# A first stage folded twice: sixteen small tiles in one round, with mirrored rows

## The chip, the core and the metric

The kernel runs on one core of a Trainium2 chip (trn2). The metric is the device time of one execution in microseconds (us); less is better. A core has TensorE (PE in the profile, with its weight loads as PEld), VectorE (DVE), ScalarE (ACT), GpSimd (POOL) and SyncE (SP). Each engine works off its own instructions in the order in which the program gives them, and semaphores make one wait for another. POOL and SP also issue DMA transfers.

## The reference

```python
# x: (8, 3008, 256), filt_r and filt_i: (1505, 256)
X = np.fft.rfft(x, axis=1)
Y = X * (filt_r + 1j * filt_i)[None]
y = np.fft.irfft(Y, n=3008, axis=1)          # per batch and channel
h = y.reshape(24064, 256) @ w_in             # w_in: (256, 2048)
g = 0.5 * h * (1.0 + erf(h / sqrt(2)))
out = g @ w_out                              # w_out: (2048, 256), out: (24064, 256)
```

So each of the 8 batches goes through a Fourier transform along its 3008 rows, a product with a filter, and the transform back; then all 24064 rows (tokens) go through two dense layers with a GELU between them.

## The kernel before

**The transform.** 3008 is 47 x 64. Row number 64 n + w of a batch is row n (0 to 46) at column w (0 to 63). The first stage (`s1`) transforms over n for every w, the second (`s2`) over w with the twiddle factors in its tables; the product with the filter (`s2_out`, `s2_sum`, VectorE) comes next, and `s3` and `s4` transform back. Between stages the data change their layout through DRAM: `s1` writes R1, `r1` loads b_sb from it; `s3_out` writes R2, `r2` loads d_sb from it, and `s4` writes y into a ring that holds two batches.

**The first stage before.** `load_x_pairs` brings w and w + 32 of a batch into x_sb, in two partition groups of 47 rows (from partitions 0 and 64), with the rows of the second half turned by 23. `fold` (lines 109 and 110) adds and subtracts the two halves, 1024 elements per partition and operation, so that even and odd outputs need one real table each, T1s. `s1` runs four times a batch (c = 0 to 3), each time as eight matmuls with 47 rows, 64 columns of weights and 512 columns of data, into four PSUM banks: one of the tag h, three of the tag f. Two of the banks are copied out by VectorE (line 327), two by ScalarE (line 325).

**The dense layers.** Tokens go in 47 blocks of 512 (`NT`). For block t, `mm1` makes 16 products of 128 hidden columns x 512 tokens (line 640, two matmuls each), in a ring of three PSUM banks of tag h, and ScalarE applies the GELU (line 643). The second layer of the block before, `mm2_seven`, uses Strassen's seven products in place of eight: 112 matmuls of 128 columns (line 714), seven per slot. VectorE forms the sums that it needs: `sums_1` (line 685, four a block), `sums_2` (line 691, two) and `sums_3` (line 696, two), and adds its results out of two PSUM banks of tag o (lines 729 to 743); POOL sends them to the output (line 761).

**The order.** The program is written out by hand in slots, 16 to a block; a slot is one `mm1` (two matmuls) and seven matmuls of `mm2_seven`. `put(slot, f, ...)` places the steps of the next batch's transform between them; a step is issued ahead of its slot's matmuls. Batch b's tokens start in block b * 3008 // 512, and `hi = first(b)` is that block's first slot. For batches 3 to 6 the four groups of `s1` stand at `hi - 94 + (0, 3, 7, 11)`, for batch 7 four slots earlier; the folds stood 20, 13, 8 and 6 slots ahead of `hi - 94`. The loads of batch b + 1 are placed in the second stage of batch b (`load_next`): a small copy on POOL (`gate`) waits until VectorE has made a certain product, and the loads stand behind it in POOL's queue. `busy` and `crowd` keep `s4` off the slots of other stages.

Of the kernel before, what the change touches and what calls it, by code (L numbers as in the profile page):

```python
# [10 lines left out]
ALU = mybir.AluOpType  # L11
FP32 = mybir.dt.float32
BF16 = mybir.dt.bfloat16
# [5 lines left out]
NA, NB = 47, 64  # L19
K1 = 24  # L20
HB = 32
# [6 lines left out]
def _dram(src, off, dims):  # L28
    return dataclasses.replace(src, offset=src.offset + off, ap=[list(d) for d in dims])


class _Mix:
    def __init__(self, ctx, tc, x, filt_r, filt_i, w_in, w_out, out):
        self.tc, self.nc = tc, tc.nc
        self.x, self.filt_r, self.filt_i = x, filt_r, filt_i
        self.w_in, self.w_out, self.out = w_in, w_out, out
        self.B, self.S, self.D = x.shape
        self.DFF = w_in.shape[1]
        assert self.S == NA * NB and self.D == 256 and self.DFF == 2048
        pool = lambda name, bufs, **kw: ctx.enter_context(tc.tile_pool(name=name, bufs=bufs, **kw))  # L40
        P = bass.MemoryType.PSUM
        self.const = pool("const", 1)
        self.px = pool("px", 1)
        self.pa = pool("pa", 3)
        self.pb = pool("pb", 2)
        self.pp = pool("pp", 3)
        self.pd = pool("pd", 3)
        self.pool = pool
        self.po = pool("po", 4)
        self.py = pool("py", 1)  # L50
        self.pg = pool("pg", 2)
        self.pq = pool("pq", 1)
        self.small = pool("small", 1)
        self.dram = pool("dram", 2, space=bass.MemoryType.DRAM)
        c = self.const
        self.T1 = c.tile([2 * NA, 96], BF16, name="T1")
        self.T2p = c.tile([128, K1, 2, 2, 16], BF16, name="T2p")
        self.xs = c.tile([128, 4, 256], BF16, name="xs")
        self.U = c.tile([128, 2, 2 * HB], BF16, name="U")
        self.T4c = c.tile([96, NA, 2], BF16, name="T4c")  # L60
        self.F = c.tile([128, 2, K1, 256], BF16, name="F")
        self.Fu = c.tile([128, 2, 2, 6, 256], BF16, name="Fu")
        f = self.F.rearrange("p t k c -> p (t k c)")
        self.s4_sb = f[:, 0:2048].bitcast(FP16).rearrange("p (i n) -> p i n", i=8)
        self.v_sb = [f[:, o:o + 1024].rearrange("p (c d) -> p c d", c=2) for o in (2048, 3072)]
        self.T4a = f[0:96, 4096:7168].rearrange("p (w m) -> p w m", w=HB)
        self.w_in_sb = c.tile([128, 2, self.DFF], BF16, name="w_in_sb")
        self.w_out_sb = c.tile([128, 16, self.D], FP16, name="w_out_sb")
        self.w_sums = c.tile([128, 4, 8, 128], FP16, name="w_sums")
        self.ps, self.st = {}, {}  # L70
        self.flip = 0
# [11 lines left out]
    def load_x(self, lo=0, n=32, hs=(0, 1)):  # L83
        nc = self.nc
        if lo == 0 and 0 in hs:
            xt = self.px.tile([128, HB, 256], BF16, tag="x", name="x_sb")
            self.st[0, "x"], self.st["x1"] = xt[0:2 * NA], xt.rearrange("p (h w) c -> p h w c", h=2)
        xt, o = self.st[0, "x"], NA
        xv = self.x[0].rearrange("(n1 h w) d -> h n1 w d", h=2, w=HB)
        for w in range(lo, lo + n, 8):  # L90
            for h in hs:
                nc.gpsimd.dma_start(out=xt[h * o:h * o + NA, w:w + 8, :], in_=xv[h][:, w:w + 8, :])  # L92

    def load_x_pairs(self, b, c, h, n=1):

        xt = self.st["x1"]
        xv = self.x[b].rearrange("(n1 h w) d -> h n1 w d", h=2, w=HB)
        for v in range(2):
            for to, at, m in ((0, 23, 24), (24, 0, 23)) if h else ((0, 0, NA),):
                w = 16 * v + 4 * c  # L100
                self.nc.gpsimd.dma_start(out=xt[64 * v + to:64 * v + to + m, h, 4 * c:4 * c + 4 * n, :],  # L101
                                         in_=xv[h][at:at + m, w:w + 4 * n, :])

    def fold(self, b, c):

        x, tt = self.st["x1"], self.nc.vector.tensor_tensor
        k, n = slice(4 * c, 4 * c + 4), 64 + NA
        s = self.st[b, "s", c] = x[:, 0, 4 * c - 4:4 * c] if c else self.xs
        tt(out=s[0:n], in0=x[0:n, 0, k], in1=x[0:n, 1, k], op=ALU.add)
        tt(out=x[0:n, 1, k], in0=x[0:n, 0, k], in1=x[0:n, 1, k], op=ALU.subtract)  # L110
# [33 lines left out]
    def load_next(self, b, p, c, h):  # L144

        if b == 1 and c > 1:
            self.gate(self.st[b, "d", 0][0:1, 0, 0:1])
        else:
            self.gate(self.st[b, "p", p][0:1, p % 2, 1, 0, 0:1])
        self.load_x_pairs(b + 1, c, h)  # L150

    def load_w_in(self):
        wi = self.w_in.rearrange("(dc p) j -> p dc j", p=128)
# [178 lines left out]
    def table_1_tiles(self, g):  # L332
# [4 lines left out]
        for p in (0, 64):  # L337
            for r in (0, K1):
                v.tensor_copy(out=self.T1s[p:p + NA, r:r + K1].rearrange("p (u c m) -> p u c m", c=4, m=2),
                              in_=self.T1[0:NA, r:r + K1].rearrange("p (c u m) -> p u c m", u=3, m=2))  # L340

    def table_2_parities(self):

        t = self.T2.rearrange("p k r (s j e) -> p k r s j e", s=2, e=2)
        for odd in range(2):
            for d in range(2):
                for q in range(2):
                    self.nc.gpsimd.tensor_copy(out=self.T2p[64 * d:64 * d + 64, odd::2, :, q, :],
                                               in_=t[0:64, odd::2, :, q, :, odd ^ d ^ q])
# [150 lines left out]
    def r2(self, b, c):  # L500
        d = self.pd.tile([96, 8, 256], BF16, tag="d", name="d_sb")
        self.st[b, "d", c] = d
        R2 = self.st[b, "R2"].rearrange("(r w) u a k m c -> r (u a k m) w c", r=2)
        for r in range(2):
            self.nc.sync.dma_start(out=d[r * 48:r * 48 + 48, :, :], in_=R2[r][:, 8 * c:8 * c + 8, :])


    def s4(self, b, grp, half, eng):
# [274 lines left out]
def kernel(  # L783
# [9 lines left out]
    m = _Mix(ctx, tc, x, filt_r, filt_i, moe_w_in, moe_w_out, out)  # L793
    nc, B, S = tc.nc, m.B, m.S
# [3 lines left out]
    g = m.small  # L798
    wide = ctx.enter_context(ExitStack())
    m.psum(wide, w=(2, 1), m=(1, 1), n=(5, 1))  # L800
    act = "act"
# [108 lines left out]
    at = {}  # L910

    def put(slot, f, *a):
        at.setdefault(slot, []).append((f, a))

    def first(b):
        return (b * S // TCH) * 16

    busy, crowd, after = set(), set(), {}
    for b in range(1, B):
        hi = first(b)  # L920
        e = 4 * (b == B - 1)
        s1, n1, r1 = (4, 3.3, 17) if b == 1 else (hi - 87, 3.7, hi - 73) if b == 2 else (hi - 94 - e, 3.7, hi - 80 - e)
        s2 = (27, 41, 54) if b == 1 else (hi - 74, hi - 59, hi - 44) if e else (hi - 64 + (b == 2), hi - 48, hi - 32)
        busy.update(range(s1 - 1, s1 + int(3 * n1) + 2))
        for c in range(4):
            slot = (4, 8, 11, 13)[c] if b == 1 else s1 + int(c * n1)
            put((0, 1, 5, 8)[c] if b == 1 else (70, 74, 86, 94)[c] if b == 2 else hi - 94 - (20, 13, 8, 6)[c], m.fold, b, c)
            put(slot, m.s1, b, c)
        for u in range(3):
            put(r1 if u < 2 else s2[0] + 1, m.r1, b, u)  # L930
            put(s2[u], m.s2, b, u)
            for i in range(4):
                put(s2[u] + 2 * i + (b == 2 and u == 0), m.s2_out, b, u, i // 2, i % 2)
            for i in range(2):
                put(s2[u] + (9 + i if 1 < b < B - 1 else 7 + 2 * i), m.s2_sum, b, 2 * u + i)
            s3 = s2[u] + ((11, 11, 12)[u] if b == 1 else 12 if e or (b, u) in ((2, 0), (B - 2, 2)) else 13)
            put(s3, m.s3, b, u)
            put(s3 + 1, m.s3_out, b, u, 1)
            busy.update(range(s2[u] - 1, s2[u] + 5), range(s3 - 1, s3 + 2))
        after[b] = s3 + 4  # L940
        crowd.update(range(s2[0], after[b]), range(s1 + 66, s1 + 94))
        if b + 1 < B:
            for i, (u, o, p) in enumerate(((0, 5, 1), (0, 7, 1), (1, 1, 2), (1, 5, 3), (1, 7, 3), (2, 1, 4), (2, 5, 5), (2, 7, 5))):
                put((76, 77, 80, 81)[i - 4] if b == 1 and i > 3 else s2[u] + o, m.load_next, b, p, i // 2, i % 2)
# [27 lines left out]
    put(9, m.table_u_pick, g)  # L972
    put(9, m.table_4_rows, g)
    put(9, m.weights_4, g)
    put(23, m.table_u)
    put(49, m.table_4_factors, g)
    for t, slot in ((3, 67), (5, 98)):
# [17 lines left out]
    for s in range((NT + 1) * 16):  # L995
        t, jc = s // 16, s % 16
# [3 lines left out]
        if t - 1 in seven:  # L1000
            n = lambda i: (14 * i if i < 3 else 42 + 70 * (i - 3) // 13) if t == late else 7 * i
            m.mm2_seven(t - 1, n(jc), n(jc + 1))
        elif t < 2:
            n = lambda i: max(4 * i - 40, 0) if i < 16 else min(24 + 8 * (i - 16) // 3, 64)
# [36 lines left out]
```

## Time and profile before

| | us |
|---|---|
| timed runs, median of 3 | 733.9 (733.84 to 733.96) |
| profiled execution, span of its instructions (the page gives no whole time for it) | 732.0 |
| PE busy | 713.6 |
| DVE busy | 597.0 |
| ACT busy | 576.5 |
| POOL busy | 286.2 |

The span runs from the first to the last instruction of one profiled execution. Rows of the profile name a line of the kernel, the engine, the operation, the tile written and the tiles read. "busy" is the time in which at least one instruction of the engine was being executed; a time in square brackets is idle time just before an instruction, with what ended it. Instructions overlap, so that the time from one start to the next can be shorter than an instruction's own duration: the first is what it takes of its engine's queue.

The first stage's matmuls (line 429) are 224, for seven batches (batch 0 goes another way), with a median of 376 ns each; they start between 39.2 and 562.0 us. The first stages of batches 3 to 7 begin at 199.5, 288.2, 377.1, 465.7 and 550.6 us.

### The profile page before, as it was taken

The numbers are of one execution on the slowest core, as the hardware profiler recorded it, in microseconds if no ns is written. First come the engines' busy times: TensorE is split into PE (matmuls) and PEld (weight loads), VectorE is DVE, ScalarE is ACT, GpSimd is POOL, SyncE is SP. The second block draws the span as 40 slices with busy tenths as digits, with TensorE's granted clock in tenths as the row PEclk, the third lists the DMA queues.
The fourth block names the chain that finished last, engine by engine and source line by source line (L and its number), as shares of the span: only waits on it lengthen the run. The fifth ranks groups of instructions, "written<-read, shape, count | busy, mean of one in ns | idle before, by whom it ended". The sixth has DMA issues, their size and how long they took to land.

```text
span 732.0 us, 22073 instructions
## 1 busy us (share of the span) xinstructions
PE 713.6 (97%) x9016; PEld 505.9 (69%) x9165; DVE 597.0 (82%) x1091; ACT 576.5 (79%) x1050; POOL 286.2 (39%) x546
## 2 busy tenths in 40 slices
PE   7999999999999999999999999999999999999997
PEld 4846675676777666666677667666677767777776
DVE  8975698899878998798976999779988897775666
ACT  7997778688877888778887788877888788877773
POOL 7853377864223452135511364115531121121121
PEclk9999999999999999999999999999999999999999
DMA  9886544765355553646535455355545442411011
GB/s 158 160 173 161 155 89 123 201 124 100 88 169 143 120 112 107 178 99 134 128 107 162 114 132 119 97 149 151 110 102 135 141 117 84 114 47 42 30 59 59
DMA packets 81254, 87.72 MB, mean 120 GB/s; under 512 B 13393, under 2 KB 61137, under 8 KB 81153
## 3 DMA queue, kind: packets, MB, share of 16 engines
q0 software_dynamic: 22288, 39.50, 24.3%
q1 hardware_dynamic: 58449, 46.62, 23.8%
q8 instruction: 71, 1.16, 0.7%
q14 instruction: 30, 0.25, 0.1%
q10 hardware_dynamic: 416, 0.20, 0.1%
HBM read 54.00 MB, written 46.66 MB: 138 GB/s over the span
## 4 chain that ended last, share of the span: by engine, by line
PE 86%; DVE 4%; DMA 4%; issue 2%; POOL 2%; ACT 1%; DVEq 0%; POOLq 0%; ACTq 0%
PE ps_o L714 38%; PE ps_h L640 38%; PE ps_s L514 3%; PE ps_o L656 2%; PE ps_s L429 2%; PE ps_s L487 2%; DMA x_sb<-in_x_dram 2%; PE ps_s L456 2%; DVE s_sb L685 1%; DMA w_out_sb<-in_moe_w_out_dram 1%; POOL F L137 1%; DMA F<-in_filt_i_dram 1%; ACT g_sb L643 1%; DVE p L467 1%; POOL x_sb L92 1%
## 5 line engine op out<-in xcount | busy, mean ns | idle before, releaser
L643 ACT ACTIVATE g_sb<-ps_h 128x512 f16<-128x512 f32 x752 | 446.4, 601 | 139.9 <-PE ps_h L640 115.5
L640 PE MATMUL ps_h<-y_sb,w_in_sb 128*128 128x512 bf16 (+3 forms) x1455 | 415.0, 365 | 1.5 <-DVE p L467 0.7
L761 POOL DMA_DIRECT2D out_dram<-ost x231 | 131.4, 575 | 388.0 <-DVE ost L743 361.3
L714 PEld LDWEIGHTS <-g_sb 128*128 128x128 f16 x2816 | 184.4, 98 | 80.7 <-issue 14.6
L640 PEld LDWEIGHTS <-w_in_sb 128*128 128x128 bf16 x1600 | 126.3, 98 | 8.3 <-issue 2.4
L714 PE MATMUL ps_o<-w_sums,g_sb 128*128 128x128 f16 x1408 | 121.7, 219 | 1.7 <-DVE g_sb L691 0.2
L714 PE MATMUL ps_o<-w_sums,s_sb 128*128 128x128 f16 x1408 | 121.2, 219 | 1.6
L714 PEld LDWEIGHTS <-s_sb 128*128 128x128 f16 x1408 | 95.1, 98 | 37.6 <-issue 2.5
L685 DVE TENSOR_TENSOR s_sb<-g_sb 128x1024 f16<-128x1024 f16 x176 | 116.4, 692 | 0.4 <-ACT g_sb L643 0.3
L714 PE MATMUL ps_o<-w_out_sb,g_sb 128*128 128x128 f16 x1408 | 113.7, 219 | 1.8
L467 DVE TENSOR_TENSOR p<-ps_s,Fu 128x1024 bf16<-128x1024 f32 x84 | 101.5, 1216 | 9.1 <-PE ps_s L456 6.5
L101 POOL DMA_DIRECT2D x_sb<-in_x_dram x156 | 79.4, 515 | 3.1 <-issue 1.6
L691 DVE TENSOR_TENSOR g_sb<-s_sb,g_sb 128x1024 f16<-128x1024 f16 x88 | 60.3, 687 | 1.5
L714 PE MATMUL ps_o<-w_out_sb,F 128*128 128x128 f16 x704 | 60.6, 219 | 0.9
L696 DVE TENSOR_TENSOR F<-g_sb 128x1024 f16<-128x1024 f16 x88 | 61.4, 697 | 0.0
L714 PEld LDWEIGHTS <-F 128*128 128x128 f16 x704 | 47.1, 98 | 14.6 <-issue 0.4
L736 DVE TENSOR_TENSOR t_sb<-t_sb,ps_o 128x256 f32<-128x256 f32 x44 | 18.4, 417 | 39.0 <-PE ps_o L714 38.6
L514 PEld LDWEIGHTS <-d_sb 96*128 96x128 bf16 x448 | 31.4, 97 | 26.8 <-issue 1.3
L325 ACT ACTIVATE F<-ps_s 128x512 bf16<-128x512 f32 x83 | 45.5, 607 | 0.1
L325 ACT ACTIVATE y_sb<-ps_s 128x376 bf16<-128x376 f32 x95 | 45.4, 478 | 0.1
L327 DVE CAST a_sb<-ps_s 128x512 bf16<-128x512 f32 x54 | 34.7, 684 | 12.0 <-PE ps_s L429 11.7
L743 DVE TENSOR_TENSOR ost<-t_sb,ps_o 128x256 f32<-128x256 f32 x86 | 32.1, 414 | 13.7 <-PE ps_o L714 13.7
(160 smaller groups left out, 589.2 us busy)
## 6 DMA issues: line engine op xcount, KB each, us to landing
out_dram<-ost POOLq DMA_DIRECT2D x127, 128.0 KB, 2.9
b_sb<-R SPq DMA_DIRECT2D x21, 512.0 KB, 5.1
R<-F SPq DMA_DIRECT2D x84, 128.0 KB, 2.5
d_sb<-R SPq DMA_DIRECT2D x56, 192.0 KB, 4.3
R<-a_sb SPq DMA_DIRECT2D x108, 96.0 KB, 2.2
x_sb<-in_x_dram POOLq DMA_DIRECT2D x48, 94.0 KB, 2.7
x_sb<-in_x_dram POOLq DMA_DIRECT2D x48, 48.0 KB, 2.8
x_sb<-in_x_dram POOLq DMA_DIRECT2D x12, 188.0 KB, 5.0
```

The source lines that it names most:

```text
L101: self.nc.gpsimd.dma_start(out=xt[64 * v + to:64 * v + to + m, h, 4 * c:4 * c + 4 * n, :], in_=xv[h][at:at + m, w:w + 4 * n, :])
L325: self.nc.scalar.activation(out=out, in_=in_, func=AF.Copy, scale=1.0 if scale is None else scale)
L327: self.nc.vector.tensor_copy(out=out, in_=in_)
L467: v(out=w[:, a], in0=ps.unsqueeze(2).to_broadcast([128, 2, 2, 256]), in1=f.unsqueeze(1).to_broadcast([128, 2, 2, 256]), op=ALU.mult)
L514: nc.tensor.matmul(ps[:, 94 * i:94 * i + 94], lhsT=d[:, (grp % 2) * 4 + i, 128 * half:128 * half + 128], rhs=self.T4a[:, 4 * grp + i, 0:2 ...
L640: nc.tensor.matmul(ps[:, o:o + n], lhsT=w[:, dc], rhs=self.ring[:, dc, off:off + n], start=(dc == 0), stop=(dc == 1))
L643: nc.scalar.activation(out=self.st["g", t][:, jc, :], in_=ps, func=AF.Gelu)
L685: self.nc.vector.tensor_tensor(out=self.st["s", t][:, i:i + 2], in0=a, in1=b, op=ALU.subtract)
L691: self.nc.vector.tensor_tensor(out=a21[:, k], in0=self.st["s", t][:, k, 0], in1=a22[:, k], op=ALU.add)
L696: self.nc.vector.tensor_tensor(out=self.s4_sb[:, k], in0=a12[:, k], in1=s2[:, k], op=ALU.subtract)
L714: nc.tensor.matmul(ps[:, (m + 1) % 2, sub, :], lhsT=a[:, i, 128 * sub:128 * sub + 128], rhs=b[:, i], start=i == 0, stop=i == 7)
L761: eng.dma_start(out=out, in_=tile_[lo - r0:lo - r0 + n])
```

## The change

In batches 3 to 7 the input of the first stage is folded twice. Besides w and w + 32, rows n and 47 - n are added and subtracted, so that 24 rows in place of 47 go into a matmul, and sums and differences go into different halves of the outputs (cosine and sine rows of the table, T1m; row 0 counts half).

For that x_sb holds four partition groups of 24 rows (from partitions 0, 32, 64 and 96), and per group the rows themselves and the mirrored rows. `turn_x` copies the batch's upper or lower rows in mirrored order from the input into a DRAM tile xr, converted to bf16, with three DMAs issued by POOL two slots ahead of the second stage of the batch before. `load_x_mirror` then issues one load of direct rows on POOL, behind the gate, and one load of mirrored rows from xr on SP, which no gate holds; eight times a batch. This replaces 24 loads a batch on POOL. Once, ahead of batch 3's loads, partitions 94 and 95 are filled from the input.

`fold_mirror` runs eight times a batch in place of the eight operations of `fold`: two operations write a sum and a difference into fold_t, a part of the tile F that the filters no longer need, and two write their sums and differences back to x_sb, for each half of the columns. Each handles 120 partitions and 2048 elements. They stand 15, 13, 11, 9, 6 and 3 slots ahead of the first group of `s1`, in its own slot, behind it, and 3 slots after.

`s1_mirror` issues 16 matmuls per group, with 24 rows, 32 columns of weights and 512 columns of data, one for each 32 x 32 tile of the array, into four banks (one h, three f), copied out as before; R1 is written by four DMAs a group as before, of other shape. The table T1m is made by eleven small operations on POOL at slot 9. The first load of d_sb in batch 6 goes in two halves. Batches 0 to 2 keep their first stage.

```diff
     def load_x(self, lo=0, n=32, hs=(0, 1)):
...
+            self.px_x = xt
...
+            self.st["xm"] = xt.rearrange("p (h e w) c -> p h e w c", h=2, e=2)
...
+    def turn_x(self, b):
+        D, n = self.D, NB * self.D
+        xr = self.st["xr"] = self.dram.tile([2, K1, HB, D], BF16, tag="xr", name="xr")
+        for h, to, at, m in ((0, 0, 0, 1), (0, 1, 46, 23), (1, 0, 23, 24)):
+            src = _dram(self.x, b * self.S * D + at * n + HB * h * D, [[8 * D, 4], [-n, m], [1, 8 * D]])
+            self.nc.gpsimd.dma_start(out=xr[h, to:to + m].rearrange("p (i w) c -> i p (w c)", w=8), in_=src)
+
+    def load_x_mirror(self, b, q, h):
+        D, n, p = self.D, NB * self.D, slice(32 * q, 32 * q + K1)
+        to = [self.st["xm"][p, h, e].rearrange("p (i e) c -> p i (e c)", e=2) for e in range(2)]
+        src = _dram(self.x, b * self.S * D + 23 * h * n + (HB * h + 2 * q) * D, [[n, K1], [8 * D, 4], [1, 2 * D]])
+        self.nc.gpsimd.dma_start(out=to[0], in_=src)
+        src = self.st["xr"][h].rearrange("p (i q e) c -> q p i (e c)", i=4, e=2)[q]
+        self.nc.sync.dma_start(out=to[1], in_=src)
+
+    def fold_mirror(self, b, k, i):
+        x, t, n = self.st["xm"][:, :, :, 4 * k:4 * k + 4], self.fold_t, 96 + K1
+        op = ALU.subtract if i % 2 else ALU.add
+        o, a0, a1 = (t[0:n, i], x[0:n, 0], x[0:n, 1]) if i < 2 else (x[0:n, :, i - 2], t[0:n, :, 0], t[0:n, :, 1])
+        self.nc.vector.tensor_tensor(out=o, in0=a0, in1=a1, op=op)
+
+    def s1_mirror(self, b, i):
...
+        ps = [self.bank("ps_s1", "f" if q else "h") for q in range(4)]
+        for d in range(2):
+            for t in range(2):
+                for q in range(4):
+                    p, o = slice(32 * q, 32 * q + K1), 64 * d + 32 * t
+                    nc.tensor.matmul(ps[q][o:o + 32, :], lhsT=self.T1m[p, t], rhs=x[p, d, t, 2 * i:2 * i + 2, :],
+                                     start=True, stop=True)
+        for q in range(4):
+            self._evac(at[:, 2 * q:2 * q + 2, :].rearrange("p w c -> p (w c)"), ps[q], "act" if q % 2 else False)
...
-        self.load_x_pairs(b + 1, c, h)
+        if b < 2:
+            self.load_x_pairs(b + 1, c, h)
+            return
...
+        self.load_x_mirror(b + 1, c, h)
...
+        n = 4 if c == 0 and b == self.B - 2 else 8
+        for w in range(0, 8, n):
+            for r in range(2):
+                self.nc.sync.dma_start(out=d[r * 48:r * 48 + 48, w:w + n, :], in_=R2[r][:, 8 * c + w:8 * c + w + n, :])
...
-            put((0, 1, 5, 8)[c] if b == 1 else (70, 74, 86, 94)[c] if b == 2 else hi - 94 - (20, 13, 8, 6)[c], m.fold, b, c)
+            if b > 2:
+                for i in range(2):
+                    put(s1 - (15, 13, 11, 9, 6, 3, 0, -3)[2 * c + i], m.fold_mirror, b, c // 2, c % 2 * 2 + i)
+                put(slot, m.s1_mirror, b, c)
+                continue
+            put((0, 1, 5, 8)[c] if b == 1 else (70, 74, 86, 94)[c], m.fold, b, c)
...
+        if 1 < b < B - 1:
+            put(s2[0] - 2, m.turn_x, b + 1)
...
+    put(9, m.table_1_mirror, g)
```

More of the change, by code (lines that the diff above doesn't have):

```diff
@@ L65, in __init__ @@
         self.v_sb = [f[:, o:o + 1024].rearrange("p (c d) -> p c d", c=2) for o in (2048, 3072)]
+        self.fold_t = f[:, 8192:12288].rearrange("p (d e w c) -> p d e w c", d=2, e=2, w=4)
         self.T4a = f[0:96, 4096:7168].rearrange("p (w m) -> p w m", w=HB)
@@ new lines, in fold_mirror @@
+    def fold_mirror(self, b, k, i):
[4 more added lines that the diff above has]
+    def s1_mirror(self, b, i):
+        nc, x = self.nc, self.st["xm"]
+        if i == 0:
+            self.st[b, "R1"] = self.dram.tile([NB, 48, 256], BF16, tag="R1", name="R1")
+        at = self.pa.tile([128, 8, 256], BF16, tag="a", name="a_sb")
+        ps = [self.bank("ps_s1", "f" if q else "h") for q in range(4)]
[7 more added lines that the diff above has]
+            self._evac(at[:, 2 * q:2 * q + 2, :].rearrange("p w c -> p (w c)"), ps[q], "act" if q % 2 else False)
+        for d in range(2):
+            for t in range(2):
+                o, w = 64 * d + 32 * t, HB * d + 8 * i
+                nc.sync.dma_start(out=self.st[b, "R1"].rearrange("n q c -> q n c")[K1 * t:K1 * t + K1, w:w + 8],
+                                  in_=at[o:o + K1])
@@ L149, in load_next @@
             self.gate(self.st[b, "p", p][0:1, p % 2, 1, 0, 0:1])
-        self.load_x_pairs(b + 1, c, h)
+        if b < 2:
+            self.load_x_pairs(b + 1, c, h)
+            return
+        if b == 2 and c == h == 0:
+            n = NB * self.D
+            self.nc.gpsimd.dma_start(out=self.px_x[94:96].rearrange("p w c -> p (w c)"),
+                                     in_=_dram(self.x, 0, [[n, 2], [1, HB * self.D]]))
+        self.load_x_mirror(b + 1, c, h)
     def load_w_in(self):
@@ L340, in table_1_tiles, with table_1_mirror @@
                               in_=self.T1[0:NA, r:r + K1].rearrange("p (c u m) -> p u c m", u=3, m=2))
+    def table_1_mirror(self, g):
+        v = self.nc.gpsimd
+        self.T1m, half = g.tile([128, 2, 32], BF16, name="T1m"), g.tile([128, 1], FP32, name="half")
+        v.memset(half, 1.0)
+        v.memset(half[0:1], 0.5)
+        v.memset(self.T1m, 0.0)
+        for p in range(0, 128, 32):
+            for r in range(2):
+                v.tensor_scalar(out=self.T1m[p:p + K1, r, 0:K1].rearrange("p (u c m) -> p u c m", c=4, m=2),
+                                in0=self.T1[0:K1, K1 * r:K1 * r + K1].rearrange("p (c u m) -> p u c m", u=3, m=2),
+                                scalar1=half[0:K1], scalar2=None, op0=ALU.mult)
     def table_2_parities(self):
@@ L503, in r2 @@
         R2 = self.st[b, "R2"].rearrange("(r w) u a k m c -> r (u a k m) w c", r=2)
-        for r in range(2):
-            self.nc.sync.dma_start(out=d[r * 48:r * 48 + 48, :, :], in_=R2[r][:, 8 * c:8 * c + 8, :])
+        n = 4 if c == 0 and b == self.B - 2 else 8
+        for w in range(0, 8, n):
+            for r in range(2):
+                self.nc.sync.dma_start(out=d[r * 48:r * 48 + 48, w:w + n, :], in_=R2[r][:, 8 * c + w:8 * c + w + n, :])
     def s4(self, b, grp, half, eng):
```

## The prediction

> **What bounds the kernel now.** I read the page first, then the chain that ended last, the waits, TensorE's timeline around one first stage, and VectorE's timeline in the same stretch.
>
> ```profile
> PE 713.6 (97%) x9016; PEld 505.9 (69%) x9165; DVE 597.0 (82%) x1091; ACT 576.5 (79%) x1050; POOL 286.2 (39%) x546
> ...
> PE 86%; DVE 4%; DMA 4%; issue 2%; POOL 2%; ACT 1%; DVEq 0%; POOLq 0%; ACTq 0%
> ```
>
> TensorE holds 86% of the chain. VectorE is next at 82% busy. The page warns that a busy PE need not be PE at its peak, so the timeline decides:
>
> ```profile
> 294.70 0.59 PE L640 MATMUL ps_h<-y_sb,w_in_sb 128*128 128x512 bf16 x2
> 295.23 0.63 PE L429 MATMUL ps_s<-x_sb,T1s 47*64 47x512 bf16 x8
> 295.79 0.56 PE L714 MATMUL ps_o<-w_sums,s_sb 128*128 128x128 f16 x7
> 296.19 0.59 PE L640 MATMUL ps_h<-y_sb,w_in_sb 128*128 128x512 bf16 x2
> 296.62 0.55 PE L714 MATMUL ps_o<-w_sums,s_sb 128*128 128x128 f16 x7
> ```
>
> This is batch 4. A plain slot is two L640 and seven L714: 0.43 + 0.39 = 0.82 us, with no idle, and these rows show no releaser. A first-stage group adds 0.10 us in front (295.23 - 294.70 - 0.43) and 0.56 us until the next L714. So in mid-kernel TensorE time is kernel time, one for one, unless it comes to wait for somebody. The first to be waited for would be VectorE:
>
> ```profile
> 288.22 0.69 DVE L691 TENSOR_TENSOR g_sb<-s_sb,g_sb 128x1024 f16<-128x1024 f16 x1
> 288.83 1.28 DVE L327 CAST a_sb<-ps_s 128x512 bf16<-128x512 f32 x2
> 290.03 0.41 DVE L729 COPY t_sb<-ps_o 128x256 f32<-128x256 f32 x1
> 291.78 1.29 DVE L327 CAST a_sb<-ps_s 128x512 bf16<-128x512 f32 x2 [1.34 <-PE ps_s L429]
> ...
> 295.73 1.29 DVE L327 CAST a_sb<-ps_s 128x512 bf16<-128x512 f32 x2 [0.68 <-PE ps_s L429]
> 297.81 0.42 DVE L736 TENSOR_TENSOR t_sb<-t_sb,ps_o 128x256 f32<-128x256 f32 x1 [0.79 <-PE ps_o L714]
> ```
>
> Here VectorE waits for TensorE, but by little: from 275 to 299 its pauses add up to 0.57 + 1.14 + 1.34 + 0.68 + 0.79 = 4.5 us.
>
> **TensorE, removed and added.** Before, a group is two rounds of four matmuls with 512 columns. In the group at 288.15 the rounds start at 288.15 and 288.39, and the next L714 at 288.71: 0.24 us for the first round, 0.32 us for the second and its tail. After, it is one round of sixteen 24x32 tiles. No row shows sixteen at once; the bounds are near. The second stage starts eight tiles (64*32, each at most 0.28 us) inside 0.30 us, so eight starts take about 0.02 us and sixteen about 0.05 us. Then the group takes 0.05 + 0.32 = 0.37 us in place of 0.56, a gain of 0.19 to 0.20 us. If starts cost nothing it is 0.24. The 0.10 us in front stays. Four groups in each of five batches: 20 x 0.197 = **3.9 us**, 0.79 us a batch. That the third stage runs four row tiles into four banks at once speaks for concurrency:
>
> ```profile
> 358.08 0.64 PE L487 MATMUL ps_s<-p,U 32*64 32x256 bf16 x32
> 358.65 0.45 PE L714 MATMUL ps_o<-w_sums,g_sb 128*128 128x128 f16 x5
> ```
>
> Its 32 matmuls need 0.57 us, four rounds of eight.
>
> The evictions of a group are unchanged: two by VectorE, 1.20 us of queue (288.83 to 290.03), and two by ScalarE. The Trainium skill, "TensorEngine Tiling (Array Packing)", section PSUM Bottleneck, says against this change that tiling speeds up TensorE but not the PSUM evacuation, which may become the limit. What it would make of the time is rival E.
>
> **VectorE, removed and added.** Out go eight folds a batch over 1024 elements, 0.69 us each; a pair holds the queue 0.72 + 0.60 = 1.32 us, the batch 5.3 us. In come eight over 2048. Three L685 in a row take 1.89 us with 0.68 for one, so one of 1024 elements holds the queue 0.60 us; L473 and L474 with 512 elements follow each other by 0.34 (532.91, 533.25). That is 0.26 to 0.27 per 512 elements, so 2048 hold it 0.60 + 0.53 = 1.13 us, the batch 9.1 us: **3.8 us more a batch**. Bounds: 1.06, with nothing fixed, and 1.42, twice the listed 0.709 mean. I take 1.13, because the rows nearest to it are queues of like operations.
>
> Where does it fall? The folds stand at slots -15, -13, -11, -9, -6, -3, 0 and +3 around the first group, so five to six of them in the 24 us whose pauses sum to 4.5 us. I follow the queue of batch 4 in the changed program's order with the durations above. It is level at 275.5 with the first eviction of the output bank. Folds one and two end at 277.7, L696 at 278.3, L731 and L734 at 279.1, fold three 280.3, L696 280.9, fold four 282.0, L736 to L740 283.2, fold five 284.3, two L685 285.5, fold six 286.7, L685 287.3, two L743 287.9 (before: 286.9), L691, L685, L691 289.8. Evictions of group 0 run from 289.8 (before: 288.83), fold seven ends at 292.1, L729 292.5, evictions of group 1 293.7, fold eight 294.8, L696, L731, L734, L696 296.8, evictions of group 2 from 296.8 (before: 295.73) to 298.0. Then it is level again. So VectorE has no pause for about 20 us and runs up to 1.9 us late.
>
> Who waits for that? Group 1 (due at 291.1) needs a bank that VectorE frees at 291.1; group 2 (due 294.8) needs fold eight, written at 294.9; the third L640 after group 2 (due 297.3) needs the h bank freed at 297.5. Each waits 0.05 to 0.15 us, 0.3 us together; bounds 0 and 0.8. Net gain 0.79 - 0.3 = **0.5 us for each of batches 3 to 6**, whose slots lie alike within the 16 of a token block.
>
> Batch 7 begins 4 slots earlier, so that its folds fall at slots 15, 1, 3, 5, 8, 11, 14 and 1 of the blocks. The same count from 536.6 has no pause at all. Fold eight ends at 557.8, where group 2 is due at 557.5; and the second L691, which stands behind it, ends at 559.2, where the product that reads it is due at 558.3. With two waits of 0.15 us that is 1.5 us (bounds 0.4 and 2.3), so batch 7 **loses 0.7 us**.
>
> **Transfers and the other queues.** Nothing else reaches the path by this count. POOL issues 24 loads of 0.515 us less and 11 more, of some 0.58 as its widest stores; it waits 361 us for stores anyway. The table's eleven small operations (about 0.2 us each, 2.2 us) fall into the 6.88 us in which POOL waits before 63.8 us. SP gets eight issues of 0.45 us; behind them stand the R2 writes and d_sb loads. They read xr, which POOL writes after the stores at 303 to 306 us (batch 4); SP cannot reach its first mirrored load before the second stage at 316 us. If xr took over 10 us, R2 would be late by the rest. xr adds 0.8 MB written and 0.8 MB read per batch to DMA engines at 0.3 to 0.65 busy. The first fold now needs all sixteen loads. For batch 7 the last is issued near 531.2 and lands, at 2.8 us, near 534; the fold is due at 536.6. Other batches have 7 us to spare. The halved d_sb load of batch 6 carries the same bytes.
>
> **Sum.** The page gives the profiled execution's span, 732.0 us; the timed runs have a median of 733.9, so 1.9 us lie outside the span, or in the difference between runs, and I carry them over. -4 x 0.5 + 0.7 = -1.3: 730.7 in span, **732.6 timed**. With all waits at their bounds the case runs from 730.4 to 735.4.
>
> **Rivals.**
> A, the full gain: VectorE's lag stays inside the buffers, the mid-block batches keep 0.7 to 0.79 us and batch 7 loses nothing. 729.9 to 731.2. For it: in batches 3 to 6 no margin is missed by over 0.15 us. Against: three places in a row, and batch 7. 0.18.
>
> B, VectorE becomes the bound: a fold holds the queue 1.25 us or more. The point from which it decides is about 1.22; beyond, h banks and output banks are late too. At 1.30 I count +0.4 us in each of four batches and +2.4 in the last: 737.9. Against: the three L685. 0.14. The Trainium skill, "VectorE: DVE Perf Modes", section Side-by-side, gives 1.22 us for 2048 elements in the 2x mode. Read as queue time, that would make the batches -0.2 each and the last +1.6: 734.7. But the rows' 0.68 for one against 0.60 in a queue say that such a number holds a tail that overlaps. I give that reading 0.03.
>
> C, the mirrored rows come late: the first fold waits at the head of VectorE's queue. A landing of 5 us, as the 188 KB loads have, in place of 2.8 just fits batch 7; 6 us costs it some 0.7; xr late by 2 us everywhere costs 10: 733 to 743. 0.05, slower.
>
> D, sixteen tiles do not run together: four rounds of 0.21 and the tail make 1.2 us a group, 20 x 0.6 more: 746. Against: L487. 0.02.
>
> E, the gain is lost at the evictions: each group hands its 0.2 us back, because the bank that is needed next comes as much later. Batches 3 to 6 gain nothing and batch 7 loses its 0.7: 734.6. Against: VectorE waited 1.34 and 0.68 us before these evictions; for it: the folds use up those pauses. 0.04.
>
> **Chances.** A measurement here can tell about 0.2%, 1.5 us, from no change. The forecast case has 0.54 and lies across that bound, at 732.4: 0.26 faster, 0.27 same, 0.01 slower. A adds 0.18 to faster; the skill's reading 0.03, E 0.04 and B 0.01 to same; B 0.13, C 0.05 and D 0.02 to slower. Faster 0.44, same 0.35, slower 0.21. The range leaves out the lowest edge of A and the worst of B, C and D: 730.0 to 736.0.
>
> **What would show it.** In the profile after: groups of x16 with the next L714 about 0.37 us behind; folds 1.13 us apart where two follow each other; no VectorE pause between 283 and 297 us of batch 4's stretch; evictions of groups 0 to 2 waiting for VectorE, not for TensorE; TensorE gaps before group 2, largest in batch 7. Folds over 1.22 us apart, a fold that waits for a DMA, or groups over 0.5 us would prove me wrong.

## The result and the profile after

The changed kernel takes 737.81 us (median of 5 runs, 736.79 to 738.59) against 733.96 us for the kernel before (5 runs, 733.84 to 734.05): a ratio of 1.0048, 95% interval 1.0038 to 1.0059. It is slower by some 3.9 us, where 732.6 us, in a range of 730.0 to 736.0 us, had been forecast. The profiled execution took 737.18 us with a span of 735.3 us; 1.9 us lie around the span, as before. So the loss is to be found inside the span, 735.3 against 732.0 us.

In the fences below, the lines of the changed kernel have other numbers: L640 became L710 (first dense layer), L714 L784 (second), L685, L691 and L696 are L755, L761 and L766 (the sums), L729, L736, L737, L740 and L743 are L799, L806, L807, L810 and L813 (the results out of the output banks), L327 is L382 (the evictions, which are the copies out of PSUM), and the stores, L761 before, are L831. So from here on L761 is a sum, in the lines of the changed kernel. New are L113 (`turn_x`), L120 and L122 (direct and mirrored loads), L129 (the folds) and L142 (the sixteen tiles).

The page of the changed kernel, busy time and the chain that ended last:

```profile
PE 721.5 (98%) x9325; PEld 506.7 (69%) x9325; DVE 614.9 (84%) x1091; ACT 576.3 (78%) x1050; POOL 262.2 (36%) x493
...
PE 85%; POOL 5%; DVE 4%; DMA 2%; ACT 2%; issue 1%; DVEq 0%; POOLq 0%; ACTq 0%
```

VectorE's share went up as forecast. What was not forecast is POOL with 5% of the chain, where it had 2%. A mark in every token block (VectorE's copy L729, now L799) shows where the two executions part. Changed kernel against before, in us:

| stretch | change |
|---|---|
| up to 143 us | -0.10 |
| the two blocks after it, 143 to 174 us (no new first stage in them) | **+2.73** |
| first stage of batch 3 / 4 / 5 / 6 | -0.77 / -0.54 / -0.76 / -0.71 |
| first stage of batch 7 | +0.67 |
| from 571 us to the last block's mark | 0.00 |
| from there to the end of the span | **+2.79** |

These add up to +3.31 us, the difference of the spans. So the first stage did bring 2.1 us; two places that the sum did not have took 5.5 us. The granted clock of the two profiles, 0.997 against 0.999, explains neither: the stretch from 571 us to the last block's mark, some 150 us of dense layers, takes the same time in both.

**The first place.** The chain that ended last, of the changed kernel, from 130 to 165 us (start, us, what):

```profile
139.33 1.22 POOL F L480
140.55 0.06 issue
140.62 1.42 POOL xr L113 x3
142.04 0.58 issue
142.62 1.13 POOL out_dram L831 x2
143.75 10.79 DMA out_dram<-ost
154.66 0.42 DVE ost L807
```

POOL builds a table (L478, L480) until 140.6 us. Then it issues batch 3's three copies into xr, and right behind them the six stores of a block. The last copy lands at 153.5 us, the first five stores one after another from 153.9 to 154.9. The store of the chain lands 10.8 us after its issue; before the change the same six stores landed after 2.0 to 3.4 us. VectorE needs its buffer back, and TensorE then waits for VectorE, as the waits say (total, times, longest):

```profile
DVE ost L807 <- DMA out_dram<-ost: 4.2, 1, 4.2
...
PE ps_o L784 <- DVE t_sb L810: 0.9, 1, 0.9
...
PE ps_o L784 <- DVE ost L813: 0.6, 1, 0.6
```

Behind L807 in VectorE's queue stand the other rows of that block, so at four places between 154 and 163 us TensorE starts its next product 1.0, 0.7, 0.6 and 0.35 us later than it would in a plain sequence.

**The second place.** Neither the page nor the chain shows it, because they count no such rows. It is in the rows of the program's last line. First the kernel before (L1036), then the changed one (L1114), as count, shortest, median and longest in ns, then first and last start:

```profile
L1036 POOLq DRAIN  x3: 46/98/4752, 723.5 to 731.7; - x3
L1036 SPq DRAIN  x3: 7/7/7, 731.2 to 731.5; - x3
```

```profile
L1114 POOLq EVENT_SEMAPHORE  x4: 17/17/17, 734.6 to 735.2; - x4
L1114 POOLq DRAIN  x3: 46/102/10485, 724.0 to 735.0; - x3
L1114 SPq DRAIN  x3: 7/7/7, 731.5 to 734.8; - x3
```

After its last store POOL executes a DRAIN, an instruction of the program's end. Before, it ran from 723.5 for 4.75 us and ended at 728.3, three us ahead of SP, which is done at 731.2. After, it starts at 724.0, takes 10.49 us, and all others, done at 731.6, wait for it until 734.5.

**What came as forecast.** TensorE in batch 4 of the changed kernel:

```profile
292.42 0.59 PE L710 MATMUL ps_h<-y_sb,w_in_sb 128*128 128x512 bf16 x2
292.94 0.45 PE L142 MATMUL ps_s<-x_sb,T1m 24*32 24x512 bf16 x16
293.33 0.56 PE L784 MATMUL ps_o<-w_sums,g_sb 128*128 128x128 f16 x7
```

The sixteen tiles take 0.39 us until the next L784 here, 0.37 us in other groups, in place of 0.56. VectorE in the same batch:

```profile
277.32 2.35 DVE L129 TENSOR_TENSOR F<-x_sb 120x2048 bf16<-120x2048 bf16 x2
279.59 0.68 DVE L766 TENSOR_TENSOR F<-g_sb 128x1024 f16<-128x1024 f16 x1
...
291.63 1.28 DVE L382 CAST a_sb<-ps_s 128x512 bf16<-128x512 f32 x2
292.83 1.22 DVE L129 TENSOR_TENSOR x_sb<-F 120x2048 bf16<-120x2048 bf16 x1
293.96 0.41 DVE L799 COPY t_sb<-ps_o 128x256 f32<-128x256 f32 x1
```

Two folds hold the queue 279.59 - 277.32 = 2.27 us, 1.135 us each (forecast 1.13), and the evictions no longer wait for TensorE.

### The profile page after: what moved, and what is told of

The parts are those of the page before. It is cut to its first block, busy times and chain, and to the rows that moved or that the text cites. A ratio compares the mean times of both kernels' runs of the same rounds, so it can differ in the third digit from the quotient of the medians.

```text
span 735.3 us, 22516 instructions
## 1 busy us (share of the span) xinstructions
PE 721.5 (98%) x9325; PEld 506.7 (69%) x9325; DVE 614.9 (84%) x1091; ACT 576.3 (78%) x1050; POOL 262.2 (36%) x493
## 3 DMA queue, kind: packets, MB, share of 16 engines
q0 software_dynamic: 25760, 39.70, 23.7%
## 4 chain that ended last, share of the span: by engine, by line
PE 85%; POOL 5%; DVE 4%; DMA 2%; ACT 2%; issue 1%; DVEq 0%; POOLq 0%; ACTq 0%
PE ps_h L710 39%; PE ps_o L784 34%; PE ps_o L726 2%; PE ps_s L584 2%; POOL tmp_sb L478 2%; PE ps_s L555 1%; PE ps_s L524 1%; DMA out_dram<-ost 1%; DVE s_sb L755 1%; POOL F L480 1%; PE ps_s L142 1%; DMA F<-in_filt_i_dram 1%; DVE p L535 1%; PE ps_c L657 1%; ACT y_sb L380 1%
## 5 line engine op out<-in xcount | busy, mean ns | idle before, releaser
L710 PE MATMUL ps_h<-y_sb,w_in_sb 128*128 128x512 bf16 (+3 forms) x1600 | 446.0, 366 | 1.0 <-DVE p L535 0.7
L831 POOL DMA_DIRECT2D out_dram<-ost x231 | 131.2, 574 | 402.1 <-DVE ost L813 371.6
L784 PEld LDWEIGHTS <-g_sb 128*128 128x128 f16 x2816 | 184.5, 98 | 81.5 <-issue 12.9
L710 PEld LDWEIGHTS <-w_in_sb 128*128 128x128 bf16 x1600 | 126.4, 98 | 8.9 <-issue 2.7
L784 PE MATMUL ps_o<-w_sums,g_sb 128*128 128x128 f16 x1408 | 122.1, 219 | 1.5 <-DVE g_sb L761 1.4
L784 PE MATMUL ps_o<-w_sums,s_sb 128*128 128x128 f16 x1408 | 121.2, 219 | 0.2 <-DVE t_sb L799 0.2
L784 PEld LDWEIGHTS <-s_sb 128*128 128x128 f16 x1408 | 95.1, 98 | 36.7 <-issue 1.5
L755 DVE TENSOR_TENSOR s_sb<-g_sb 128x1024 f16<-128x1024 f16 x176 | 116.4, 692 | 0.7 <-ACT g_sb L713 0.3
L784 PE MATMUL ps_o<-w_out_sb,g_sb 128*128 128x128 f16 x1408 | 113.9, 219 | 1.5 <-DVE t_sb L810 0.9
L761 DVE TENSOR_TENSOR g_sb<-s_sb,g_sb 128x1024 f16<-128x1024 f16 x88 | 60.4, 687 | 1.5
L766 DVE TENSOR_TENSOR F<-g_sb 128x1024 f16<-128x1024 f16 x88 | 61.4, 698 | 0.0
L784 PE MATMUL ps_o<-w_out_sb,F 128*128 128x128 f16 x704 | 60.6, 219 | 0.0
L784 PEld LDWEIGHTS <-F 128*128 128x128 f16 x704 | 47.1, 98 | 14.4 <-issue 0.2
L813 DVE TENSOR_TENSOR ost<-t_sb,ps_o 128x256 f32<-128x256 f32 x86 | 32.1, 414 | 16.5 <-PE ps_o L784 16.5
L806 DVE TENSOR_TENSOR t_sb<-t_sb,ps_o 128x256 f32<-128x256 f32 x44 | 18.3, 415 | 29.1 <-PE ps_o L784 28.4
L584 PE MATMUL ps_s<-F,d_sb 96*128 96x94 bf16 x448 | 37.2, 204 | 0.1
L382 DVE CAST a_sb<-ps_s 128x512 bf16<-128x512 f32 x54 | 34.6, 681 | 2.5 <-PE ps_s L497 2.1
```

The source lines that it names most:

```text
L382: self.nc.vector.tensor_copy(out=out, in_=in_)
L584: nc.tensor.matmul(ps[:, 94 * i:94 * i + 94], lhsT=d[:, (grp % 2) * 4 + i, 128 * half:128 * half + 128], rhs=self.T4a[:, 4 * grp + i, 0:2 ...
L710: nc.tensor.matmul(ps[:, o:o + n], lhsT=w[:, dc], rhs=self.ring[:, dc, off:off + n], start=(dc == 0), stop=(dc == 1))
L755: self.nc.vector.tensor_tensor(out=self.st["s", t][:, i:i + 2], in0=a, in1=b, op=ALU.subtract)
L761: self.nc.vector.tensor_tensor(out=a21[:, k], in0=self.st["s", t][:, k, 0], in1=a22[:, k], op=ALU.add)
L766: self.nc.vector.tensor_tensor(out=self.s4_sb[:, k], in0=a12[:, k], in1=s2[:, k], op=ALU.subtract)
```

## Experiments

Each was timed in turn with the kernel before on the same chip; ratios are to that kernel, with 95% intervals. The medians of before lay at 733.90 to 734.01 us in all of them.

**The copy for batch 3 issued earlier.**

```diff
-            put(s2[0] - 2, m.turn_x, b + 1)
+            put(54 if b == 2 else s2[0] - 2, m.turn_x, b + 1)
```

> The three L113 copies for batch 3 are issued at slot 54 (near 79 us, where POOL waits) and not at slot 111, straight ahead of the six stores of 142.6 us. Theory (the copies stand in front of the stores, a store then lands after 10.8 us and VectorE waits 4.2 us for its ost buffer): that wait is gone, the TensorE gaps between 154 and 163 us (2.7 us) too; 737.8 - 2.7 = 735.1 us. Rival (any traffic of the copies costs this, wherever they stand, or the first wait for the mirrored rows is the cause): the gaps stay or move, 737.8. The last DRAIN of POOL, 10.5 us after the last store's issue, should stay as it is by every theory, since as many copies are issued.

Measured: 734.70 us, ratio 1.0008 (1.0000 to 1.0017). POOL issues the copies at 78.9 us, and L807 starts as soon as L806 lets it:

```profile
149.94 0.41 DVE L806 TENSOR_TENSOR t_sb<-t_sb,ps_o 128x256 f32<-128x256 f32 x1
150.39 0.42 DVE L807 TENSOR_TENSOR ost<-t_sb,ps_o 128x256 f32<-128x256 f32 x1
```

The stretch that was 2.73 us longer than before is now level, to 0.01 us. The copies were not faster here: the last one lands 14.2 us after its issue, at 94.3 us, and stores issued at 87.2 to 88.4 us, while it was under way, land behind it, after 6.7 to 7.3 us. Only nobody waits for them. So stores behind the copies in POOL's queue are late in both places, and what cost 2.7 us was that at 142 us VectorE needed the buffers. The DRAIN stayed, 10.47 us.

**Only the copies, in the kernel before.** `turn_x` and its line in the plan, and nothing else of the change.

```diff
+        if 1 < b < B - 1:
+            put(s2[0] - 2, m.turn_x, b + 1)
```

> The kernel before with the 15 copies of L113 added at the slots that the change gives them; nobody reads xr. First stage and loads are the old ones. Theory (stall at batch 3 and the DRAIN both come from the copies alone): VectorE waits about 4 us for an ost buffer near 150 us, TensorE loses 2.7 us there; DRAIN near 10.5 us, 2.9 us at the end: 733.9 + 5.6 = 739.5 us. Rival for the stall (it needs the new loads behind the copies): no wait, and rival for the DRAIN (it comes from the new loads): 4.75 us; both rivals 733.9, one of them 736.6 to 736.8.

Measured: 736.43 us, ratio 1.0036 (1.0024 to 1.0049). The stall is there without any of the new loads, tiles or folds, and costs 2.59 us (L807, VectorE's row that waits for its buffer, is L745 here):

```profile
154.71 0.42 DVE L745 TENSOR_TENSOR ost<-t_sb,ps_o 128x256 f32<-128x256 f32 x1 [4.05 <-DMA out_dram<-ost]
```

From there to the end the marks stay 2.68 us behind those of before, so the copies for batches 4 to 7 cost nothing. The DRAIN is 5.99 us, not 10.5: the theory of the stall holds, the theory that the copies lengthen the DRAIN fails.

**One copy instead of five.**

```diff
-        if 1 < b < B - 1:
+        if b == 2:
             put(s2[0] - 2, m.turn_x, b + 1)
```

> Only batch 3 is copied to xr; batches 4 to 7 read batch 3's mirrored rows again, so their output is wrong. 12 of the 15 L113 copies are left out, all else stays. Theory (the copies DRAM to DRAM lengthen POOL's last DRAIN from 4.75 to 10.5 us, in proportion to their number): DRAIN 4.75 + 5.7 / 5 = 5.9 us, over before SP's end at 731.6, and the end comes 2.9 us sooner: 734.9 us. Rival (the DRAIN comes from something else, as the direct loads' new form or the kernel's end): it stays near 10.5 us, 737.8 us. The stall at 150 to 163 us stays by both.

Measured: 736.1 us, ratio 1.0026 (1.0017 to 1.0035). The DRAIN is 8.75 us: neither 5.9 nor 10.5. So with these two runs neither the copies, nor the packets (before 22288, this 22496, the changed kernel 25760, the kernel before with copies 26368) order the DRAINs. The transfers that POOL issues do, if they are counted from the last full 128:

| kernel | transfers issued by POOL | beyond a full 128 | DRAIN, us |
|---|---|---|---|
| before | 411 | 27 | 4.75 |
| before, with the copies | 426 | 42 | 5.99 |
| changed, one copy | 335 | 79 | 8.75 |
| changed (and with the early copy) | 347 | 91 | 10.49 (10.47) |

The changed kernel issues fewer transfers than the one before, since 120 loads became 40, 15 copies and one fill of two partitions, and has the longer DRAIN. A count from 64 would put 411 and 347 at the same 27. The number 128 itself was chosen to fit: counted from 120, these kernels come in the same order.

**Forty one-row transfers more.** That reading came from the same numbers that it explains, so it was put to two kernels with counts not seen yet.

```diff
+    for t in (36, 37, 38, 39):
+        put(16 * t + 2, m.small_copies, 10)
```

> The changed kernel with 40 copies of one row (1 KB read, 512 bytes written, nobody reads them) put on POOL's queue behind the stores of four late blocks, ten in each, where POOL waits 11 us for the next stores. So far POOL's last DRAIN was 4.75 us with 411 transfers issued by POOL (before), 5.99 with 426, 8.75 with 335 and 10.48 with 347. Theory (it grows with the number of transfers since the last full 128: 27, 42, 79 and 91): 387 transfers leave 3, the DRAIN falls to 2.3 to 3 us, ends before SP is done, and the kernel gains the 2.9 us of its tail: 734.9 us. Rival 1 (it grows by 0.08 to 0.14 us with each transfer, whatever the count): 14 to 16 us, 741 to 743 us. Rival 2 (it depends on the form of the transfers, the copies and direct loads): 10.5 us, 737.8 us.

Measured: 734.77 us, ratio 1.0011 (1.0002 to 1.0020). The DRAIN of this kernel:

```profile
L1123 POOLq DRAIN  x3: 50/98/4013, 724.8 to 732.9; - x3
```

4.01 us, over at 728.8 us while SP is done at 732.4. More transfers made it shorter and the kernel 3 us faster than the changed one: no growth with each transfer, and not their form. It is not as short as the 2.3 to 3 us that were expected; what sets it at so low a count is not shown.

**Sixty-four more in the kernel before.**

```diff
+    for t in (36, 37, 38, 39):
+        put(16 * t + 2, m.small_copies, 16)
```

> The kernel before with 64 such one-row copies, sixteen behind the stores of each of the same four blocks (0.55 us each, 8.8 us of the 11 us that POOL waits there). Theory of the count since the last full 128: 475 transfers leave 91, as in the changed kernel, so the last DRAIN becomes 10 to 10.5 us though none of the new loads and copies is there; it ends near 734.0 in place of 728.3, 2.8 us behind SP's end at 731.2: 736.8 us. Rival (the DRAIN comes from the new loads and the copies of mirrored rows): 4.75 us, 734.0 us.

Measured: 736.40 us, ratio 1.0030 (1.0019 to 1.0040); the difference to the blocks' marks of before moves by 0.02 us at most from 96 us to the end, and the DRAIN is

```profile
L1045 POOLq DRAIN  x3: 50/97/9974, 723.7 to 734.2; - x3
```

The tail of the changed kernel appears in a kernel that has nothing of the change: here, too, it is the number of transfers that was altered.

**Without the folds.**

```diff
-                for i in range(2):
-                    put(s1 - (15, 13, 11, 9, 6, 3, 0, -3)[2 * c + i], m.fold_mirror, b, c // 2, c % 2 * 2 + i)
```

> The changed kernel without its 40 folds (L129): the sixteen tiles read the unfolded rows, so the output of batches 3 to 7 is wrong. Theory (TensorE's gain is 0.79 us a batch, and VectorE's folds take back what is missing: about 0.4 us in batches 3 to 6 together, and 0.67 + 0.79 = 1.46 us in batch 7): 737.8 - 1.9 = 735.9 us with the stall at batch 3 and the DRAIN unchanged; batch 7's two blocks 0.79 us shorter than before in place of 0.67 longer. Rival (batch 7's loss comes from its loads, evictions or SP's queue and not from the folds): batch 7 still 0.67 longer, 737.4 or more.

Measured: 735.83 us, ratio 1.0023 (1.0015 to 1.0032). By the marks the batches now gain 0.77, 0.78, 0.76, 0.77 and 0.77 us: the whole gain of TensorE. What the folds take back is the difference to the changed kernel: 0.00, 0.24, 0.00 and 0.06 us in batches 3 to 6, and 1.44 us in batch 7.

**Batch 7: another order.** On top of the early copy.

```diff
-            slot = ... else s1 + int(c * n1)
+            slot = ... else s1 + int(c * n1) + (0, 0, e // 2, 0)[c]
-                    put(s1 - (15, 13, 11, 9, 6, 3, 0, -3)[2 * c + i], m.fold_mirror, ...
+                    put(s1 - (15, 13, 11, 9, 6, 3, 0, -3 - e // 4)[2 * c + i], m.fold_mirror, ...
```

> The kernel with the early copy, and for batch 7 alone the eighth fold one slot later (behind the second L761 in VectorE's queue) and group 2 of the first stage two slots later. Theory (the 0.74 us wait of L784 for L761, behind the eighth fold, is the main part of batch 7's loss): that wait goes, batch 7's stretch from 528 to 571 us changes from 0.67 us longer than before to between 0.3 shorter and level; 734.7 - 0.8 = 733.9 us, at best 733.3. Rival (VectorE has no time left there whatever the order, so the wait moves to group 2 or to the output bank): 0.5 or more stays, 734.5 or more. The DRAIN stays 10.5 us by every theory.

Measured: 734.34 us, ratio 1.0005 (0.9996 to 1.0014). Batch 7 is 0.37 us longer than before in place of 0.67, between the two expectations and nearer to the rival's. TensorE in that stretch:

```profile
554.92 0.51 PE L784 MATMUL ps_o<-w_sums,g_sb 128*128 128x128 f16 x6 [0.45 <-DVE g_sb L761]
...
556.38 0.22 PE L784 MATMUL ps_o<-w_sums,s_sb 128*128 128x128 f16 x1 [0.19 <-DVE t_sb L799]
```

With the fold behind it, L761 is still late, and L799, now behind the fold, is late too. This order did not remove VectorE's backlog; it moved a part of the wait.

**Batch 7: less work for VectorE, and the tail mended.** The early copy; every direct load in two halves, which makes 387 transfers; two evictions moved to ScalarE.

```diff
-        src = _dram(self.x, b * self.S * D + 23 * h * n + (HB * h + 2 * q) * D, [[n, K1], [8 * D, 4], [1, 2 * D]])
-        self.nc.gpsimd.dma_start(out=to[0], in_=src)
+        for i in (0, 2):
+            src = _dram(self.x, b * self.S * D + 23 * h * n + (HB * h + 8 * i + 2 * q) * D,
+                        [[n, K1], [8 * D, 2], [1, 2 * D]])
+            self.nc.gpsimd.dma_start(out=to[0][:, i:i + 2], in_=src)
...
-            self._evac(..., ps[q], "act" if q % 2 else False)
+            self._evac(..., ps[q], "act" if q % 2 or b == self.B - 1 and i == 1 else False)
```

> The early copy, the new first stage in all of batches 3 to 7, each direct load in two halves (387 transfers, 3 beyond a full 128), and for batch 7 the two evictions of group 1 that VectorE makes given to ScalarE: 1.2 us less on VectorE ahead of the second L761, 1.0 us more on ScalarE, whose pauses between 550 and 558 us sum to 1.05 us. Theory (batch 7's loss is VectorE's backlog, whoever takes work off it helps): L784 waits no longer for L761, batch 7 between 0.3 us longer than before and 0.5 shorter; DRAIN near 4 us: 733.9 - 2.8 + 0.3 to - 0.5 = 730.6 to 731.4 us. Rival (ScalarE then hands its GELU rows on late, so TensorE waits for g_sb or for an h bank instead): batch 7 loses 0.6 or more, 731.7 us or more.

Measured: 730.58 us (730.02 to 730.78), ratio 0.9949 (0.9936 to 0.9963): faster than both kernels. The DRAIN is 3.49 us and ends at 723.8, SP at 727.9. Batch 7 is 0.51 us shorter than before, by the theory's far end. The waits of the second layer's weight loads for the sum that was late (L761, here L763; total, times, longest) are what they were before the change, 0.7 us in two; with the early copy alone they were 1.6 us in three, 0.9 the longest:

```profile
PEld L786 <- DVE g_sb L763: 0.7, 2, 0.4
```

The halved loads and the moved evictions came together. Batch 7's part is put down to the evictions, since no fold waits for a load with the early copy alone, and in VectorE's queue the sum L763 moves up by just the 1.2 us that were taken out.

**Batch 7 on the old first stage.** The early copy and the halved loads as above, 392 transfers.

```diff
-        if b < 2:
+        if b < 2 or b == self.B - 2:
             self.load_x_pairs(b + 1, c, h)
...
-            if b > 2:
+            if 2 < b < B - 1:
...
-        if 1 < b < B - 1:
+        if 1 < b < B - 2:
             put(54 if b == 2 else s2[0] - 2, m.turn_x, b + 1)
```

> The early copy, batch 7 on the old first stage (its old loads, folds and groups, no copy for it), and each direct load of batches 3 to 6 issued in two halves, so that POOL issues 392 transfers: 8 beyond a full 128. Theory (each piece adds): no stall at batch 3; batches 3 to 6 gain 0.77, 0.54, 0.76 and 0.71 us as in the changed kernel; batch 7 level with before; the last DRAIN near 4 us as with 387 transfers, over before SP is done: 733.9 - 2.8 = 731.1 us. Rival (the tail is not the count's but the mirrored loads', or more loads on POOL cost as much as they bring): DRAIN near 10 us or a new wait at the loads, 733.5 to 734 us.

Measured: 731.49 us (731.24 to 732.28), ratio 0.9965 (0.9952 to 0.9977), DRAIN 3.60 us, batch 7 level with before to 0.01 us. With the stall at batch 3 and the tail both gone, the first stage in batches 3 to 6 brings 2.73 us by the marks.

## Why the prediction was wrong

**The step that failed** is the part on transfers and the other queues: "Nothing else reaches the path by this count." Two things did, 2.73 and 2.79 us, against 0 in the sum.

*The copies.* I followed them for batch 4 ("POOL writes after the stores at 303 to 306 us") and asked only who reads xr, and when. For batch 3 neither holds: POOL is held by its table until 140.6 us, the copies are issued ahead of the stores, and those who wait are not the readers of xr but the stores behind it, then VectorE for its buffer, then TensorE. The rows to see it with were in the profile before, where POOL's table rows end in the same place and the six stores follow at once:

```profile
139.42 1.34 POOL L412 TENSOR_TENSOR F<-tmp_sb 96x376 bf16<-96x376 f32 x1
140.71 3.40 POOL L761 DMA_DIRECT2D out_dram<-ost  x6
```

The two large copies took 14.5 and 13.9 us (medians of five). That is more than the 10 us from which the prediction counted the writes of R2 as late. They were not late in batch 4: SP issued the first two mirrored loads at 322.6 and 324.8 us and the next R2 write at 331.0. Rival C had a landing that comes late, but put the harm at the fold. The Trainium skill, "DMA: Bandwidth & Descriptors", section SWDGE vs HWDGE vs iDMA, says that GpSimd's transfers have a single queue; the 10.8 us of a store behind three copies agree with it.

*The end of the span.* "1.9 us lie outside the span ... I carry them over" held for what is outside. But the sum had no term for POOL's last DRAIN, which before was hidden by 731.2 - 728.3 = 2.9 us of cover that I did not name. The change took 64 transfers off POOL's queue, for which the prediction saw no cost, and the DRAIN grew by 5.7 us.

**The steps that held.** TensorE's gain: 0.79 us a batch forecast, 0.76 to 0.78 found without folds. The fold's hold on VectorE: 1.13 forecast, 1.135 found. VectorE's queue: in batch 4 the evictions of groups 0 and 2 were forecast for 289.8 and 296.8 us; the changed kernel is 1.86 us behind there, and they start at 291.63 and 298.61. Batch 7: a loss of 0.7 us forecast from waits of 0.3 us (group 2, for the eighth fold), 0.9 us (the product that reads the second L761) and twice 0.15, together 1.5; a loss of 0.67 found, from 1.44. Both larger waits were where the count put them. Group 2 takes 0.74 us until the next L784 in place of 0.37, and the product that reads the second L761 comes 0.9 us late, 0.74 of it idle:

```profile
557.35 0.80 PE L142 MATMUL ps_s<-x_sb,T1m 24*32 24x512 bf16 x16
558.09 0.23 PE L784 MATMUL ps_o<-w_sums,g_sb 128*128 128x128 f16 x1
559.06 0.51 PE L784 MATMUL ps_o<-w_sums,g_sb 128*128 128x128 f16 x6 [0.74 <-DVE g_sb L761]
```

**A term of the wrong size.** The waits in batches 3 to 6 were put at 0.3 us each, 1.2 together. They are 0.30 us together: 0.24 in batch 4 (a gap of 0.19 us before the third L710 behind group 2, one of the three forecast places), 0.06 in batch 6, none in 3 and 5. By the first stage alone the kernel would have gained 2.1 us where 1.3 was forecast.

**The other rivals.** A came true for batches 3, 5 and 6 but not for batches 4 and 7. B did not: the folds hold the queue for less than its 1.22 us. The Trainium skill, "VectorE: DVE Perf Modes", section Side-by-side, gives 1.22 us for 2048 elements in the 2x mode. The rows list 1.21 to 1.22 us, so the trace agrees with it as the length of one, while in a queue the next starts after 1.135. D fell with the groups of 0.37 to 0.39 us. E did not show: without folds every batch kept its 0.77 us with the evictions unchanged, so it was the folds and not the evictions that took gain back. The Trainium skill, "TensorEngine Tiling (Array Packing)", section PSUM Bottleneck, says that the copies out of PSUM may become the limit; the kept 0.77 us say that here they did not. In batch 7 moving two evictions off VectorE still helped, since all its work stands in one queue.

**What stays open.** What POOL does during its DRAIN, and what exactly is counted to 128, no row shows; the count fits all eleven kernels, which have seven different counts, but a period of 120 would order them nearly as well, so that 128 is a reading and not a measured figure. Why a copy from DRAM to DRAM takes 14 us was not taken apart.

## What to carry to other kernels

When a step adds transfers to a queue, ask for every occurrence, not for one, what stands behind them in that queue at that moment, and follow the stores as well as the readers: of the copies for five batches, those for batch 3 cost 2.7 us and the others nothing. Put a term for the end of the program into the sum: which engine is done last, and by how much the others are covered. And where an engine has a backlog, taking work off it (1.2 us here) repaired what the one other order that was tried repaired only in part.

## What the runs showed of the hardware

POOL's DRAIN at the end of the program took 3.5 to 10.5 us, and its length went with the number of transfers that POOL had issued, counted anew after each 128 or so: by 128, 3 over gave 3.49 and 4.01 us, 8 gave 3.60, 27 gave 4.75, 42 gave 5.99, 79 gave 8.75, 91 gave 9.97 to 10.49. Sixteen 24x32 tiles with 512 columns took 0.37 to 0.39 us of TensorE's time, where two rounds of four 47x64 tiles took 0.56. A copy of 368 or 384 KB from DRAM to DRAM on POOL's queue, which also converts to 16 bits, landed after 14 us, while the 188 KB loads landed after 5.4; and a store behind three such copies landed after 10.8 us.
